# Fused cosine attention and token/channel mixer on one core: moving T4 and parts of T2 to GpSimd, another place for S1's tile, norms between exponentials, and a last product in two tiles

## The chip, the core and the metric

The kernel runs on one core of a Trainium2 chip. The core has five engines with a queue each: TensorE (PE in the profile; its weight loads are PEld), VectorE (DVE), ScalarE (ACT), GpSimd (POOL) and SyncE (SP), which issues most of the transfers. An engine takes its instructions in the order of its own queue and waits for others by semaphores. Matmul results land in PSUM, eight banks of 2 KiB per partition; everything else lives in SBUF.

The metric is the device time of one execution in microseconds (us); less is better. The time of a kernel is the median of several executions.

## The reference

Inputs in fp32: q, k, v of shape 8 x 12 x 448 x 64 (batch, heads, rows, head size), tau = 0.1 and four weight matrices.

```
q_n = q / (norm(q) + 1e-6);  k_n = k / (norm(k) + 1e-6)
attn = softmax(q_n @ k_n.T / tau)                 # 448 x 448 for each of 96 heads
x = (attn @ v), heads side by side                # 8 x 448 x 768
h = relu(x.T @ w_tok1) @ w_tok2                   # 448 -> 256 -> 448, over the rows
u = x + h.T
out = u + relu(u @ w_ch1) @ w_ch2                 # 768 -> 1536 -> 768, over the channels
```

## The kernel before

**Pairs.** Attention runs over 48 pairs of heads, six for each batch. A pair's life is spread over several turns ("slots") of one loop (line 909): its rows are loaded on SP, squared on GpSimd (`squares`), summed on VectorE (`sums`, line 266), turned into norms (`norms`: Ln and Exp on ScalarE, lines 277 and 278; a sum and a reciprocal on VectorE, lines 274 and 275), scaled to fp16 on GpSimd (`scaled`, lines 298 and 306, into a `kq` tile), transposed by a transfer on SP (`tpose_dma`, line 330, `qk<-kq`), multiplied to scores (`score`, line 345), put through exponentials on ScalarE (line 346, three of 896 columns, and line 353 for the remaining rows), and multiplied with v (`pv_rest` and `pv`, lines 367 and 384, into two `psO` banks). v is cast by GpSimd (`cast_v`, line 228). Then come the two token layers (`tok1`, line 420 with its eviction `rt` at 423; `tok2`, line 434 with its eviction `u` at 437). In slot i the scores are those of pair i and the norms and the scaling those of pair i + 2.

**Channel layers.** The two channel layers of a finished batch are cut into units (lines 467 and 483), which are put between the steps of later pairs. The loop's order is written by hand: what stands in the source is the order of each engine's queue.

**The tail.** The last two batches (B0, B1) go through the channel layers together, each layer as one 2 x 2 block product in seven block products instead of eight. For this the kernel forms sums and differences of blocks: of the first weights (`fast_weights1`: s1w, s2w, s4w, and one in place), of the second weights (`fast_weights2(n, engine)`: T1 to T4, each in three pieces of 128 x 768 fp16, each read by a later sum or a product), of u (`fast_x`: t1x to t4x) and of the hidden values (`fast_g(g, 1..4)` for each of three pairs of row tiles g; line 536 for all of them, and the tile's name tells them apart: t1g to t4g, or s1g to s4g where g is 1). The first layer's products are `p1` to `p7` (line 586), its outputs are put together by VectorE and GpSimd (`c22` on GpSimd, from two fp32 tiles) and pass a ReLU in place on ScalarE (`relu`, line 629). The second layer's products are `q1` to `q7` for each g (line 671): product 2 adds to the bank of product 1, 3 to that of 5, and 7 and 4 to that of 6, each after the bank was evicted. Last come the rows that both batches share (`shared_half`, line 735), and the stores (`store_row`, line 719).

**Order of the tail's queues before.** T1 stands on GpSimd in slot 41 (line 895). S1 stands there at the end of slot 46 (line 955), S2 on VectorE in slot 47 after the x of pair 46 (line 925), S4 on GpSimd at the end of slot 47. T2 follows t4x on GpSimd (line 991), T3 follows c22(0) (line 1001), and T4 is done by VectorE between the second layer's first and second group (line 1033).

**Memory.** The tiles of the tail are taken from a pool that opens when the pool `rest` closes in slot 45 (lines 950 to 953). `rest` held the `kq` tiles, which the transposing transfers read. In the order of allocation before, s1w lies on memory of `kq`, and so its first writer waits for the last such transfer. PSUM has two pools: `ps`, two banks (tag "b"), and `ps2`, three buffers of two banks (tag "s").

Of the kernel before, what the change touches and what calls it, by code (L numbers as in the profile page):

```python
# [22 lines left out]
def kernel(  # L23
# [511 lines left out]
    def tt(eng, out, a, b, op):  # L535
        eng.tensor_tensor(out=out, in0=a, in1=b, op=op)
# [3 lines left out]

    def tail_tiles():
        fw["t"] = {k: xtile(k, "x", [128, HD, S]) for k in (1, 2)}
        fw["s"] = [tail.tile([128, HD, C // 2], FP16, name=f"s{n}w1") for n in (1, 2, 4)]

    def xtile(k, name, shape):
        return (tail if k < 3 else tail2).tile(shape, FP16, name=f"t{k}{name}", tag=f"t{k}x", bufs=1)
# [42 lines left out]
    def etile(kind, d, bufs=1):  # L589
        e[kind, d] = (tail if kind == "e1" and d == 0 else tail2).tile([128, 2, S], FP32, name=f"{kind}_{d}", tag=kind, bufs=bufs)  # L590
        return e[kind, d][:]

    def gpart(i, b, d):
# [2 lines left out]
    def p1(d):  # L596
        bank2("X", d)
        prod1(1, d, px, True)
        nc.scalar.activation(out=etile("e1", d, 2 if d else 1), in_=px[d][:, :, 0:S], func=AF.Copy)

    def p2(d):
        prod1(2, d, px, False)
# [1 line left out]

    def p5(d):
        prod1(5, d, pz, True)
        nc.scalar.activation(out=etile("e5", d, 2), in_=pz[d][:, :, 0:S], func=AF.Copy)

    def p6(d):
        prod1(6, d, py, True)  # L610
        tt(nc.vector, etile("e16", d, 2), py[d][:, :, 0:S], e["e1", d][:], ALU.add)

    def p7(d):
        prod1(7, d, py, False)
        tt(nc.vector, etile("e167", d, 2), py[d][:, :, 0:S], e["e1", d][:], ALU.add)

    def c22(d):
        tt(nc.gpsimd, gpart(1, 1, d), e["e167", d][:], e["e5", d][:], ALU.add)
# [9 lines left out]
    def relu(i, b, d):  # L628
        nc.scalar.activation(out=gpart(i, b, d), in_=gpart(i, b, d), func=AF.Relu)

    def fast_weights2(n, eng):
        def w(i, j):
            return [wc2t[:, HC * i + 2 * m:HC * i + 2 * m + 2, DH * j:DH * (j + 1)] for m in range(3)]

        t = fw.setdefault("t2", {})
        at = [(n - 1 + m) % 2 for m in range(3)]
        t[n] = [qkv.tile([128, 2, DH], FP16, name=f"t{n}w2_{m}", tag=("qf", "kf")[z]) for m, z in enumerate(at)]
        a, b = {1: (w(0, 1), w(0, 0)), 2: (w(1, 1), t.get(1)), 3: (w(1, 1), w(0, 1)), 4: (w(1, 0), t.get(2))}[n]
        for m in range(3):
            tt(eng, t[n][m][:], a[m], b[m] if n % 2 else b[m][:], ALU.subtract)  # L640

    def fast_w2(n, j):
        if n < 4:
# [2 lines left out]
        return fw["t2"][{4: 4, 5: 1, 6: 2, 7: 3}[n]][j // 2][:, j % 2]  # L646

    TILES = ((0, 1), (2, 6), (4, 5))
    sg, xo, yo, zo, eo, orow = {}, {}, {}, {}, {}, {}

    def gtile(t, i, j0=0, j1=HC):
# [29 lines left out]
    def etile2(kind, g, bufs=2):  # L681
        eo[kind, g] = tail2.tile([128, DH], FP32, name=f"{kind}_{g}", tag=kind.replace("f", "e") if kind in ("f5", "f16", "f167") else kind, bufs=bufs)
        return eo[kind, g][:]

    def q1(g):
        xo[g] = ps.tile([128, 512], FP32, name=f"psXo_{g}", tag="b")
        prod2(1, g, xo[g], True)
        nc.scalar.activation(out=etile2("f1", g, 2), in_=xo[g][:, 0:DH], func=AF.Copy)

    def f1u(g):  # L690
        tt(nc.gpsimd, j3(etile2("f1u", g, 1)), j3(eo["f1", g][:]), urow(TILES[g][1], 0), ALU.add)
# [12 lines left out]
    def q2(g):  # L704
        orow[g] = [outp.tile([128, D], FP32, name=f"orow_{g}_{n}", tag="ost") for n in range(2)]
        prod2(2, g, xo[g], False)
        tt(nc.vector, j3(orow[g][0][:, 0:DH]), j3(xo[g][:, 0:DH]), urow(TILES[g][0], 0), ALU.add)

    def q7(g):
        prod2(7, g, yo[g], False)  # L710
# [11 lines left out]
    def q3(g):  # L722
        prod2(3, g, zo[g], False)
        tt(nc.vector, orow[g][0][:, DH:D], zo[g][:, 0:DH], eo["f16", g][:], ALU.add)
        store_row(TILES[g][0], orow[g][0])

    def q4(g, lo=0, hi=DH):
        prod2(4, g, yo[g], False, lo, hi)
        tt(nc.vector, j3(orow[g][1][:, lo:hi]), j3(yo[g][:, lo:hi]), j3(eo["f1u", g][:, lo:hi]), ALU.add)

    def shared_half(h):
        lo = DH * h
        psF = ps.tile([128, 512], FP32, name=f"psF_shared_{h}", tag="b")
        for ct in range(CT):
            nc.tensor.matmul(psF[:, 0:DH], gts[B0 // 2][:, ct, 384:512], wc2t[:, ct, lo:lo + DH],
                             start=(ct == 0), stop=(ct == CT - 1))
        o = qkv.tile([128, DH], FP32, name=f"ost_shared_{h}", tag=("qf", "kf")[h])
        (c, p0, p1_), = pieces(384, S)
        for r, b, slot in ((0, B0, 3), (64, B1, 0)):
            tt(nc.vector, j3(o[r:r + 64]), j3(psF[r:r + 64, 0:DH]), u16[b][r:r + 64, HD * h:HD * (h + 1), slot], ALU.add)  # L740
        for r, b in ((0, B0), (64, B1)):
            nc.sync.dma_start(out=out[b].rearrange("(p c) d -> c p d", c=NCH)[c, p0:p1_, lo:lo + DH], in_=o[r:r + 64])
# [21 lines left out]
    with tc.manual_schedule():  # L764
# [123 lines left out]
        def side(i):  # L888
            if i + 6 < NP_ALL and i + 2 < DMA_T0:
                load_qk(i + 6)  # L890
            cast_v(i)
            if i + 3 < NP_ALL:
                squares(i + 3)
            if i == NP_ALL - 7:
                fast_weights2(1, nc.gpsimd)
            if i in (8, 11):
                weights_ch2((i - 8) // 3)
            if i + 2 < NP_ALL:
                norms(i + 2)
                norms(i + 2, dve=True)  # L900
                scaled(i + 2)
                if i + 2 >= DMA_T0:
                    tpose_dma(i + 2)
            if i + 6 < NP_ALL and i + 2 >= DMA_T0:
                load_qk(i + 6)
            if i + 4 < NP_ALL:
                load_v(i + 4)

        for i in range(NPAIR + 1, NP_ALL):
            b, pj = i // NPAIR, i % NPAIR  # L910
            for c in range(KC):
# [12 lines left out]
            if i == NP_ALL - 1:  # L924
                fast_weights1(2, nc.vector)
            if i == NPAIR + 1:
                refill(0)
            elif pj == 2 and 1 < b < B - 1:
                refill(b - 1)
            side(i)  # L930
            if i == NP_ALL - NPAIR:
                fed[1] = (sum(t for t, _ in queue) - fed[0]) / NPAIR
            fed[0] += fed[1]
            unit(True)
            if old(i):
# [99 lines left out]
        q7(0)  # L1035
        fast_g(1, 1)
        q3(0)
        fast_g(1, 2)
        q4(0)
        store_row(TILES[0][1], orow[0][1])  # L1040
        f1u(1)
        q5(1)
        fast_g(1, 3)
        q6(1)
        fast_g(1, 4)
        q2(1)
        fast_g(2, 1)
        q7(1)
        fast_g(2, 2)
        q3(1)  # L1050
        fast_g(2, 3)
        q4(1)
        store_row(TILES[1][1], orow[1][1])
        fast_g(2, 4)
        q1(2)
        f1u(2)
        q5(2)
        q6(2)
        q2(2)
# [44 lines left out]
```

## Time and profile before

| what | us |
|---|---|
| median of 3 runs | 384.05 (383.45 to 385.09) |
| the profiled execution, device time | 384.17 |
| its span, first to last instruction | 382.4 |
| slots 44 and 45, start of scores | 301.92, 306.62 |
| slots 46 and 47, start of scores | 311.69, 318.32 |
| first layer of the tail, its first product | 322.93 |
| second layer, its first product | 350.61 |
| shared rows, first matmul | 371.98 |
| last product of the kernel (128 columns) | 377.73 |
| last store issued on SP, end | 379.58 |

The stretches of the last part, from the table of engines by window (busy us in each):

| from : to | PE | DVE | ACT | POOL | DMA GB/s |
|---|---|---|---|---|---|
| 300 : 310 | 10.00 | 7.25 | 6.42 | 7.71 | 138 |
| 310 : 320 | 9.83 | 6.05 | 4.89 | 6.28 | 128 |
| 320 : 330 | 9.40 | 8.67 | 4.56 | 6.18 | 93 |
| 330 : 340 | 10.00 | 8.15 | 4.16 | 5.17 | 0 |
| 340 : 350 | 10.00 | 7.36 | 5.48 | 9.97 | 2 |
| 350 : 360 | 8.53 | 9.74 | 5.33 | 5.82 | 1 |
| 360 : 370 | 10.00 | 8.02 | 1.47 | 6.08 | 155 |
| 370 : 383 | 7.20 | 4.61 | 0.00 | 2.74 | 95 |

A row of the order of time reads: start, length, engine, line, operation, output<-input, shape, count, and in brackets how long the engine had been idle and what ended that. Lengths of rows with a count are from the first start to the last end. The granted TensorE clock is 1.00 in every stretch up to 370 us and 0.996 over the span.

### The profile page before, as it was taken

How to read it: one execution, taken by the hardware profiler on the slowest of the kernel's cores; microseconds unless marked ns; L12 is line 12 of the kernel's file. 1: busy time of each engine (PE TensorE's matmuls, PEld its weight loads, DVE VectorE, ACT ScalarE, POOL GpSimd, SP SyncE). 2: the span in 40 equal slices, each digit the busy share in tenths (PEclk: the TensorE clock that was granted, in tenths of full speed). 3: DMA queues.
4: the chain of work that ended last, by engine and by line, in shares of the span. 5: the costliest groups of instructions: out<-in, count | busy, mean ns of one | idle time of the engine just before them, and what ended most of it. 6: DMA issues, size and time to landing. Idle time of an engine off the chain costs nothing.

```text
span 382.4 us, 10261 instructions
## 1 busy us (share of the span) xinstructions
PE 366.8 (96%) x4080; PEld 239.9 (63%) x4080; DVE 247.9 (65%) x562; ACT 234.2 (61%) x400; POOL 281.5 (74%) x411
## 2 busy tenths in 40 slices
PE   7888999989999999999999999999999999999894
PEld 6466666666667666667656666666666666655552
DVE  7789766776436574557445674556545767887973
ACT  5999887846665457845675466764676564436310
POOL 8999798978667577678567767758789867299561
PEclk9999999999999999999999999999999999999998
DMA  7999999999996898979796898967977764100234
GB/s 199 258 254 176 231 233 191 248 223 152 200 225 136 168 208 196 196 181 178 186 205 128 194 184 205 177 174 182 208 175 137 144 153 88 44 0 3 65 107 119
DMA packets 116256, 64.35 MB, mean 168 GB/s; under 512 B 72304, under 2 KB 112880, under 8 KB 116208
## 3 DMA queue, kind: packets, MB, share of 16 engines
q1 hardware_dynamic: 110224, 58.21, 72.2%
q0 software_dynamic: 5616, 5.21, 8.6%
q8 instruction: 32, 0.52, 0.6%
q10 hardware_dynamic: 368, 0.28, 0.2%
q14 instruction: 16, 0.13, 0.2%
HBM read 43.45 MB, written 11.01 MB: 142 GB/s over the span
## 4 chain that ended last, share of the span: by engine, by line
PE 78%; DVE 6%; POOL 5%; DMA 4%; ACT 3%; issue 2%; POOLq 0%; SPq 0%; DVEq 0%; ACTq 0%
PE psG L467 21%; PE psF L483 18%; PE psO L384 9%; PE psS L345 7%; PE psU L434 5%; PE psR L420 5%; PE psY L586 3%; DMA qk<-kq 2%; POOL kq L298 2%; ACT pt L346 2%; PE psYo L671 2%; PE psQ L352 2%; PE psZ L586 1%; PE psX L586 1%; DVE ssq L266 1%
## 5 line engine op out<-in xcount | busy, mean ns | idle before, releaser
L346 ACT ACTIVATE pt<-psS 128x896 f16<-128x896 f32 (+1 forms) x156 | 132.4, 917 | 53.3 <-PE psS L345 53.3
L483 PE MATMUL psF<-wc2t,gt 128*128 128x384 f16 x504 | 88.4, 326 | 0.0
L467 PE MATMUL psG<-ut,wc1t 128*128 128x448 f16 x432 | 88.1, 352 | 0.0
L298 POOL TENSOR_TENSOR kq<-kf,rn 128x384 f16<-128x384 f32 (+1 forms) x47 | 41.8, 888 | 61.5 <-DVE rn L275 59.3
L483 PEld LDWEIGHTS <-gt 128*128 128x128 f16 x504 | 47.1, 98 | 27.8
L467 PEld LDWEIGHTS <-wc1t 128*128 128x128 f16 x432 | 40.2, 98 | 32.4
L470 ACT ACTIVATE gt<-psG 128x448 f16<-128x448 f32 x72 | 38.8, 539 | 33.2 <-PE psG L467 33.2
L266 DVE TENSOR_REDUCE ssq<-sq 128x15 f32<-128x960 f32 (+2 forms) x51 | 56.2, 1102 | 3.5 <-ACT sq L248 1.9
L423 DVE TENSOR_SCALAR rt<-psR 128x256 f16<-128x256 f32 x48 | 20.1, 418 | 50.8 <-PE psR L420 50.8
L298 POOL TENSOR_TENSOR kq<-qf,rn 112x512 f16<-112x512 f32 x45 | 47.0, 1043 | 3.0
L345 PE MATMUL psS<-qk 64*128 64x448 f16 x312 | 41.7, 357 | 5.0 <-DVE qk L324 3.0
L250 POOL TENSOR_TENSOR sq<-kf 128x384 f32<-128x384 f32 (+1 forms) x46 | 40.1, 872 | 1.7 <-DMA kf<-in_k_dram 1.7
L487 DVE TENSOR_TENSOR ost<-psF,u 128x384 f32<-128x384 f32 (+1 forms) x48 | 25.6, 533 | 24.3 <-PE psF L483 21.7
L250 POOL TENSOR_TENSOR sq<-qf 112x512 f32<-112x512 f32 x39 | 40.5, 1038 | 0.0
L384 PE MATMUL psO<-vt,pt 128*128 128x65 f16 (+1 forms) x1024 | 39.2, 193 | 0.0
L388 DVE TENSOR_TENSOR x<-psO,rec 128x256 f16<-128x256 f32 x82 | 34.8, 425 | 2.8
L384 PEld LDWEIGHTS <-pt 128*128 128x128 f16 (+1 forms) x1024 | 34.2, 97 | 3.5 <-issue 0.9
L437 DVE TENSOR_TENSOR u<-psU,x 128x512 f16<-128x512 f32 x48 | 32.3, 674 | 1.9 <-PE psU L434 0.5
L434 PE MATMUL psU<-rt,w2t 128*128 128x128 f16 x384 | 29.3, 219 | 0.5 <-POOL w2t L198 0.5
L434 PEld LDWEIGHTS <-w2t 128*128 128x128 f16 x384 | 24.8, 98 | 7.9 <-issue 0.8
L420 PEld LDWEIGHTS <-w1t 128*128 128x128 f16 x384 | 24.8, 98 | 7.9 <-issue 1.8
L420 PE MATMUL psR<-x,w1t 128*128 128x128 f16 x384 | 29.3, 219 | 0.2 <-DVE u L437 0.2
(128 smaller groups left out, 477.1 us busy)
## 6 DMA issues: line engine op xcount, KB each, us to landing
qf<-in_q_dram SPq DMA_DIRECT2D x47, 224.0 KB, 4.4
kf<-in_k_dram SPq DMA_DIRECT2D x36, 192.0 KB, 3.8
vf<-in_v_dram SPq DMA_DIRECT2D x36, 192.0 KB, 3.7
vf<-in_v_dram SPq DMA_DIRECT2D x12, 224.0 KB, 8.5
kf<-in_k_dram SPq DMA_DIRECT2D x11, 224.0 KB, 8.7
wc1t<-in_moe_w_ch_dram POOLq DMA_DIRECT2D x4, 576.0 KB, 11.6
wc2t<-in_moe_w_ch_dram POOLq DMA_DIRECT2D x2, 1152.0 KB, 14.1
out_dram<-ost SPq DMA_DIRECT2D x6, 336.0 KB, 3.5
```

The lines of the kernel that those rows point to most:

```text
L250: nc.gpsimd.tensor_mul(out=dst, in0=src, in1=src)
L266: nc.vector.tensor_reduce(out=st["ssq"][0:n, sl], in_=st["sq"][0:n, sl], axis=AXX.X, op=ALU.add)
L298: eng.tensor_tensor(out=kq[0:p, a, 0:n].rearrange("p c g e -> p g c e"), in0=st["kq"[a]][:].rearrange("p (g c) e -> p g c e", g=2), in1=_b ...
L345: nc.tensor.matmul(psS[:, hh, 0:S], qk[hb, c * n:c * n + 128], qm[hb], start=True, stop=True)
L346: nc.scalar.activation(out=pts[i % 2][0:n, 2 * S * c:2 * S * (c + 1)].rearrange("p (h s) -> p h s", h=2), in_=psS[0:n, :, 0:S], func=AF.Ex ...
L384: nc.tensor.matmul(psO[:, m, 0:E + 1], pts[i % 2][0:n, at:at + 128], vt[0:n, i % HP, nch * hh + c, 0:E + 1], start=(old(i) and c == 0), st ...
L388: nc.vector.tensor_tensor(out=st["x"][:, :, hh * E:(hh + 1) * E], in0=psO[:, :, 0:E], in1=_bcast_free(rec[:], E), op=ALU.mult)
L420: nc.tensor.matmul(psR[:, tt], w1t[:, w1[m], tt * 128:(tt + 1) * 128], st["x"][:, m], start=(m == 0), stop=(m == 3))
L434: nc.tensor.matmul(psU[:, m], w2t[:, tt, lo:lo + 128], st["rt"][:, tt], start=(tt == 0), stop=(tt == TT - 1))
L467: nc.tensor.matmul(psG[:, 0:S], wc1t[:, dt, ct * 128:(ct + 1) * 128], ut[b][:, dt].rearrange("p m s -> p (m s)")[:, lo:lo + S], start=(dt ...
L470: nc.scalar.activation(out=gt[:, ct, (b % 2) * S:(b % 2 + 1) * S], in_=psG[:, 0:S], func=AF.Relu)
L483: nc.tensor.matmul(psF[:, 0:hi - lo], gt[:, ct, at:at + 128], wc2t[:, ct, lo:hi], start=(ct == 0), stop=(ct == CT - 1))
```

## The change

Five edits, all from slot 42 on:

- **T4 and T2.** `fast_weights2` loses its engine (always GpSimd) and can do single pieces. T2's first piece goes into slot 45, ahead of the scaling of pair 47; its second to the end of slot 46, ahead of S1; its third stays behind t4x. T3 follows at once, ahead of c22(0). T4 goes from VectorE to GpSimd, between c22(0) and c22(1).
- **S1's tile.** The tile e1_0 (fp32, 128 x 896) is taken from the tail's pool ahead of the S tiles, so they all move along. In the built program S1 then waits for its weights alone.
- **Norms.** In slots 42 to 45 the two ScalarE steps of the norms of pair i + 2 go from the side work after the three exponentials to a place between the second and the third. VectorE's two steps stay.
- **Order of the second layer.** Product 1 of group 1 goes ahead of product 5 of group 0. The groups become a loop: sums of the next group stand between the products of this one, and each sum goes one place ahead of the eviction that follows. The shared halves move from "b" to "s" buffers.
- **The last product.** In group 2, product 2 becomes the last of the kernel instead of product 4, and it runs in two tiles (256 and 128 columns), each with a bank of its own; product 1 of group 2, which fills these banks first, is cut likewise. Product 4 of group 2 stands between the shared halves and stores whole rows; products 3 and 7 trade places.

```diff
 def tail_tiles():
     fw["t"] = {k: xtile(k, "x", [128, HD, S]) for k in (1, 2)}
+    fw["e1"] = tail.tile([128, 2, S], FP32, name="e1_0", tag="e1")
     fw["s"] = [tail.tile([128, HD, C // 2], FP16, name=f"s{n}w1") for n in (1, 2, 4)]
...
-def fast_weights2(n, eng):
+def fast_weights2(n, parts=range(3)):
...
-    for m in range(3):
-        tt(eng, t[n][m][:], a[m], b[m] if n % 2 else b[m][:], ALU.subtract)
+    for m in parts:
+        tt(nc.gpsimd, t[n][m][:], a[m], b[m] if n % 2 else b[m][:], ALU.subtract)
...
+ENDS = ((0, 256), (256, DH))
...
-def q1(g):
-    xo[g] = ps.tile([128, 512], FP32, name=f"psXo_{g}", tag="b")
-    prod2(1, g, xo[g], True)
-    nc.scalar.activation(out=etile2("f1", g, 2), in_=xo[g][:, 0:DH], func=AF.Copy)
+def q1(g, cuts=((0, DH),)):
+    f1 = etile2("f1", g)
+    for lo, hi in cuts:
+        xo[g, lo] = ps.tile([128, 512], FP32, name=f"psXo_{g}_{lo}", tag="b")
+        prod2(1, g, xo[g, lo], True, lo, hi)
+        nc.scalar.activation(out=f1[:, lo:hi], in_=xo[g, lo][:, lo:hi], func=AF.Copy)
...
-    psF = ps.tile([128, 512], FP32, name=f"psF_shared_{h}", tag="b")
+    psF = ps2.tile([128, 512], FP32, name=f"psF_shared_{h}", tag="s")
...
         if i == NP_ALL - 7:
-            fast_weights2(1, nc.gpsimd)
+            fast_weights2(1)
+        if i == NP_ALL - 3:
+            fast_weights2(2, (0,))
...
         if i + 2 < NP_ALL:
-            norms(i + 2)
+            if i < NP_ALL - 6:
+                norms(i + 2)
             norms(i + 2, dve=True)
             scaled(i + 2)
...
         for c in range(KC):
             score(i, c)
+            if c == 1 and NP_ALL - 6 <= i < NP_ALL - 2:
+                norms(i + 2)
...
         if i == NP_ALL - 2:
+            fast_weights2(2, (1,))
             fast_weights1(1, nc.gpsimd)
...
     fast_x(3, 2, 3)
-    fast_weights2(2, nc.gpsimd)
+    fast_weights2(2, (2,))
+    fast_weights2(3)
...
     relu(1, 1, 0)
-    fast_weights2(3, nc.gpsimd)
+    fast_weights2(4)
...
     fast_g(0, 3)
+    q1(1)
+    relu(1, 1, 1)
     q5(0)
-    relu(1, 1, 1)
     relu(0, 1, 2)
     relu(1, 1, 2)
     q6(0)
     fast_g(0, 4)
-    q1(1)
-    fast_weights2(4, nc.vector)
-    q2(0)
-    q7(0)
-    fast_g(1, 1)
-    q3(0)
-    fast_g(1, 2)
-    q4(0)
...
+    for g in range(2):
+        rows(g)
+        q2(g)
+        fast_g(g + 1, 1)
+        q7(g)
+        fast_g(g + 1, 2)
+        q3(g)
+        store_row(TILES[g][0], orow[g][0])
+        fast_g(g + 1, 3)
+        q4(g)
+        fast_g(g + 1, 4)
+        if g == 0:
+            f1u(1)
+        else:
+            q1(2, ENDS)
+            f1u(2)
+        q5(g + 1)
+        q6(g + 1)
+    rows(2)
     q3(2)
+    store_row(TILES[2][0], orow[2][0], DH, D)
     q7(2)
-    store_row(TILES[2][1], orow[2][1], DH, D)
     shared_half(0)
+    q4(2)
     shared_half(1)
-    q4(2, 0, 256)
-    store_row(TILES[2][1], orow[2][1], 0, 256)
-    q4(2, 256, DH)
-    store_row(TILES[2][1], orow[2][1], 256, DH, nc.scalar)
+    for (lo, hi), eng in zip(ENDS, (nc.sync, nc.scalar)):
+        q2(2, lo, hi)
+        store_row(TILES[2][0], orow[2][0], lo, hi, eng)
```

`rows(g)` is new and only takes the two output tiles of a group; `q2` and `q4` change with it (`q2` gets the column range that `q4` had).

More of the change, by code (lines that the diff above doesn't have):

```diff
@@ L587, in prod1, with etile @@
                                  start=(start and j == 0), stop=(j == HD - 1), skip_group_check=True)
-    def etile(kind, d, bufs=1):
-        e[kind, d] = (tail if kind == "e1" and d == 0 else tail2).tile([128, 2, S], FP32, name=f"{kind}_{d}", tag=kind, bufs=bufs)
+    def etile(kind, d):
+        first = kind == "e1" and d == 0
+        e[kind, d] = fw["e1"] if first else tail2.tile([128, 2, S], FP32, name=f"{kind}_{d}", tag=kind, bufs=2)
         return e[kind, d][:]
@@ L598, in p1 @@
         prod1(1, d, px, True)
-        nc.scalar.activation(out=etile("e1", d, 2 if d else 1), in_=px[d][:, :, 0:S], func=AF.Copy)
+        nc.scalar.activation(out=etile("e1", d), in_=px[d][:, :, 0:S], func=AF.Copy)
     def p2(d):
@@ L606, in p5 @@
         prod1(5, d, pz, True)
-        nc.scalar.activation(out=etile("e5", d, 2), in_=pz[d][:, :, 0:S], func=AF.Copy)
+        nc.scalar.activation(out=etile("e5", d), in_=pz[d][:, :, 0:S], func=AF.Copy)
     def p6(d):
         prod1(6, d, py, True)
-        tt(nc.vector, etile("e16", d, 2), py[d][:, :, 0:S], e["e1", d][:], ALU.add)
+        tt(nc.vector, etile("e16", d), py[d][:, :, 0:S], e["e1", d][:], ALU.add)
     def p7(d):
         prod1(7, d, py, False)
-        tt(nc.vector, etile("e167", d, 2), py[d][:, :, 0:S], e["e1", d][:], ALU.add)
+        tt(nc.vector, etile("e167", d), py[d][:, :, 0:S], e["e1", d][:], ALU.add)
     def c22(d):
@@ L635, in fast_weights2 @@
         t = fw.setdefault("t2", {})
-        at = [(n - 1 + m) % 2 for m in range(3)]
-        t[n] = [qkv.tile([128, 2, DH], FP16, name=f"t{n}w2_{m}", tag=("qf", "kf")[z]) for m, z in enumerate(at)]
+        if n not in t:
+            at = [(n - 1 + m) % 2 for m in range(3)]
+            t[n] = [qkv.tile([128, 2, DH], FP16, name=f"t{n}w2_{m}", tag=("qf", "kf")[z]) for m, z in enumerate(at)]
         a, b = {1: (w(0, 1), w(0, 0)), 2: (w(1, 1), t.get(1)), 3: (w(1, 1), w(0, 1)), 4: (w(1, 0), t.get(2))}[n]
-        for m in range(3):
-            tt(eng, t[n][m][:], a[m], b[m] if n % 2 else b[m][:], ALU.subtract)
+        for m in parts:
+            tt(nc.gpsimd, t[n][m][:], a[m], b[m] if n % 2 else b[m][:], ALU.subtract)
     def fast_w2(n, j):
@@ L702, in q6, with rows, q2 @@
         tt(nc.gpsimd, j3(eo["f5", g][:]), j3(eo["f5", g][:]), urow(TILES[g][1], 1), ALU.add)
-    def q2(g):
+    def rows(g):
         orow[g] = [outp.tile([128, D], FP32, name=f"orow_{g}_{n}", tag="ost") for n in range(2)]
-        prod2(2, g, xo[g], False)
-        tt(nc.vector, j3(orow[g][0][:, 0:DH]), j3(xo[g][:, 0:DH]), urow(TILES[g][0], 0), ALU.add)
+    def q2(g, lo=0, hi=DH):
+        prod2(2, g, xo[g, lo], False, lo, hi)
+        tt(nc.vector, j3(orow[g][0][:, lo:hi]), j3(xo[g, lo][:, lo:hi]), urow(TILES[g][0], 0)[:, lo // 128:hi // 128], ALU.add)
     def q7(g):
@@ L724, in q3, with q4 @@
         tt(nc.vector, orow[g][0][:, DH:D], zo[g][:, 0:DH], eo["f16", g][:], ALU.add)
[L725 to L729, printed above, removed]
+    def q4(g):
+        prod2(4, g, yo[g], False)
+        tt(nc.vector, orow[g][1][:, 0:DH], yo[g][:, 0:DH], eo["f1u", g][:], ALU.add)
+        store_row(TILES[g][1], orow[g][1])
     def shared_half(h):
         lo = DH * h
-        psF = ps.tile([128, 512], FP32, name=f"psF_shared_{h}", tag="b")
+        psF = ps2.tile([128, 512], FP32, name=f"psF_shared_{h}", tag="s")
         for ct in range(CT):
@@ L1031 @@
         fast_g(0, 4)
-        q1(1)
-        fast_weights2(4, nc.vector)
-        q2(0)
-        q7(0)
-        fast_g(1, 1)
-        q3(0)
-        fast_g(1, 2)
-        q4(0)
[L1040 to L1059, printed above, removed]
+        for g in range(2):
[17 more added lines that the diff above has]
+        rows(2)
         q3(2)
+        store_row(TILES[2][0], orow[2][0], DH, D)
         q7(2)
-        store_row(TILES[2][1], orow[2][1], DH, D)
         shared_half(0)
+        q4(2)
         shared_half(1)
-        q4(2, 0, 256)
-        store_row(TILES[2][1], orow[2][1], 0, 256)
-        q4(2, 256, DH)
-        store_row(TILES[2][1], orow[2][1], 256, DH, nc.scalar)
+        for (lo, hi), eng in zip(ENDS, (nc.sync, nc.scalar)):
+            q2(2, lo, hi)
+            store_row(TILES[2][0], orow[2][0], lo, hi, eng)
 _INS = ['q', 'k', 'v', 'tau', 'moe_w_tok1', 'moe_w_tok2', 'moe_w_ch1', 'moe_w_ch2']
```

## The prediction

> **What bounds the kernel now.** I read the totals first, then TensorE's waits by window, then the order of time where the waits lie.
>
> ```profile
> span 382.4 us, 10261 instructions
> PE 366.8 (96%) x4080; PEld 239.9 (63%) x4080; DVE 247.9 (65%) x562; ACT 234.2 (61%) x400; POOL 281.5 (74%) x411
> PE psYo L671 <- DVE f L536: 1.1, 1, 1.1
> PE psYo L671 <- DVE orow L536: 1.0, 1, 1.0
> PE psO L367 <- DVE u L437: 0.5, 1, 0.5
> PE psZo L671 <- DVE t1g L536: 0.4, 1, 0.4
> PE psS L345 <- DMA qk<-kq: 0.2, 1, 0.2
> ```
>
> TensorE is busy for 96% of the span, so only its waits can be won. The five rows of waits are all that it has from 300 us on; they are single events and end 3.2 us of idle time. The end of a matmul in the trace lies some 0.16 us behind the time at which the next could start (six products of 384 columns start every 0.97 us in the chain of waits, yet the last shows as busy for 0.326), so each stall in the second layer is about 0.15 us larger than its row.
>
> ```profile
> 316.65 4.54 POOL L536 TENSOR_TENSOR s1w<-wc1t 128x2304 f16<-128x2304 f16 x1 [2.97 <-DMA qk<-kq]
> 321.14 0.50 POOL L228 CAST vt<-vf 128x384 f16<-128x384 f32 x1
> 321.22 1.63 DVE L536 TENSOR_TENSOR s2w<-s1w,wc1t 128x2304 f16<-128x2304 f16 x1 [0.31 <-POOL s1w L536]
> 324.68 0.61 PE L367 MATMUL psO<-vt,pt 64*128 64x65 f16 x8 [0.46 <-DVE u L437]
> 335.82 4.84 POOL L536 TENSOR_TENSOR t2w<-wc2t,t1w 128x768 f16<-128x768 f16 x3
> 347.54 4.13 POOL L536 TENSOR_TENSOR gt<-e,e 128x896 f16<-128x896 f32 x2
> 350.75 1.34 DVE L536 TENSOR_TENSOR t1g<-gt 128x768 f16<-128x768 f16 x1
> 352.13 0.56 DVE L536 TENSOR_TENSOR t2g<-t1g,gt 128x768 f16<-128x768 f16 x1
> 355.32 2.93 DVE L536 TENSOR_TENSOR t4w<-wc2t,t2w 128x768 f16<-128x768 f16 x3
> 359.24 1.14 PE L671 MATMUL psYo<-t4w,gt 128*128 128x384 f16 x6 [1.06 <-DVE f L536]
> 377.26 0.42 DVE L536 TENSOR_TENSOR orow<-psYo,f1u 128x256 f32<-128x256 f32 x1
> 377.73 0.49 PE L671 MATMUL psYo<-t4w,gt 128*128 128x128 f16 x6 [1.03 <-DVE orow L536]
> 377.87 1.71 SPq L719 DMA_DIRECT2D out_dram<-orow  x3
> 378.27 0.29 DVE L536 TENSOR_TENSOR orow<-psYo,f1u 128x128 f32<-128x128 f32 x1 [0.59 <-PE psYo L671]
> 378.59 0.34 ACTq L719 DMA_DIRECT2D out_dram<-orow  x1
> ```
>
> The reader is to see four places: GpSimd's 2.97 us in front of S1, VectorE's T4 (2.93 us) in front of the 1.06 us wait, the two tiles of one bank at the end, and three stores behind each other on SP.
>
> **Norms between the exponentials: 0.2 us.** In pairs 42 to 45 the Ln (0.32) and the Exp of the norm (0.22) run ahead of the third exponential, so the norms come one exponential (0.81) earlier and that exponential 0.65 later. GpSimd starts to scale pair 46 that much sooner, its transpose lands sooner, and the 0.2 us wait for `qk<-kq` goes (bounds 0 and 0.25). What hides the later exponential: in slot 43 it would end at 298.6, and TensorE takes its bank back at 299.43. The Ln would be asked for at 308.63 in slot 45, where VectorE's sum (307.22, 1.14) has ended at 308.36; margins in the other slots are 0.28 to 0.43. Behind a waiting Ln stand the third exponential and `psQ`'s. Cover gone, it costs TensorE up to the whole delay (second rival).
>
> **S1, with T2's first two pieces: 0.7 us.** One T piece is 4.84/3 = 1.61 us on GpSimd. Piece 0 now stands ahead of pair 47's scaling. Before, GpSimd idled 1.30 us there (casts end 309.28, scaling starts 310.58); with norms 0.8 sooner the casts end at 308.5, the piece at 310.1, the scaling (2.66) at 312.8 where it was 313.24. Its transpose on SP goes no later; even 1.3 us later it would be hidden, since it landed at 316.5 for scores that start at 318.32. Then the cast of v (0.46), piece 1 and S1 (4.54): S1 ends at 319.4 where it ended at 321.19. It no longer waits for the transpose, nor does anything on GpSimd behind it. S2 on VectorE stands behind the x of pair 46, which ends at 320.91; before, it had to let the cast of 321.14 pass (to 321.64) and ended at 322.85. Now it can run at 320.91 and end 0.7 us sooner. Behind it are two evictions, u (324.63) and rt (324.96), which free the two banks of `psO`. Product 1 ends at 322.93 + 6 x 0.19 = 324.07; `psO` started at 324.68 and took 0.61 against 0.30 in the slot before, so TensorE lost 0.61 + 0.31 = 0.92. With both evictions 0.7 sooner, the first bank is free in time (323.93) and the second 0.2 late: gain 0.7. Bounds: 0.3 (only VectorE's own 0.31 goes) and 0.92. e1's tile takes the memory that S1 leaves; its copy comes at 324, 7 us after the last transpose landed, and is hidden.
>
> **T4 on GpSimd, and product 1 of the second rows ahead of product 5: 1.2 us.** GpSimd runs from t4x (334.83) to the last c22 (351.67) without a gap. Two of T2's pieces leave this stretch, T4's three come in: one piece more. T2's last and T3's three now stand ahead of c22(0), so each c22 ends 1.61 later: 344.3, 351.2, and the last 353.3. Who waits: ReLUs on ScalarE and, behind them, the copies e5(1) and e5(2). They ended at 347.25 and 348.38, would end at 347.8 and 348.7, and products 3 want them at 348.34 and 349.48: hidden by 0.5 to 0.8 us; beyond that TensorE waits for every further us.
>
> Then VectorE's t1g. Its 1.34 us against 0.55 ended 0.42 after the second c22 did (351.67): two fp16 operands from SBUF stand still while GpSimd runs. T4's rows say the same: beside GpSimd's pair of additions two pieces took 1.27, the one after it 0.55. So t1g, ready at 350.75, runs when c22(1) ends, 351.2 to 351.63; c22(2) follows to 353.7, and t2g is held until then and ends at 354.1. TensorE: product 1 at 350.61, product 1 of the second rows at 351.58, product 5 at 352.56 (t1g in time, its stall of 0.57 gone), product 6 asked for at 353.53 and started at 354.15: a new stall of 0.6. Products 2, 7 and 3 follow in 0.975 each, and product 4 starts at 354.15 + 4 x 0.975 = 358.05, if the eviction of 7 is done by then; with 2.93 us of T4 gone VectorE has it at about 357.9. It was 359.24, with the same seven products before it: gain 1.2. Bounds: 1.8 if t2g slips in ahead of c22(2), 0.5 if the ReLUs of c22(2) also hold group 1's first sum, and by it the eviction of product 7, for 0.7. From product 4 to the shared rows both kernels have 17 times 0.975 us, and six more matmuls (256 + 128 columns for 384) cost nothing.
>
> The Trainium skill (SBUF — State Buffer, "Who interferes with whom") has a rule against this part: a VectorE tensor_tensor with both inputs in SBUF and a GpSimd instruction that reads SBUF exclude each other for the whole instruction. The t1g row agrees (1.34 for 0.55); if that row were only slowed by sharing, t2g would end at 353.0, no stall would come, and the sum would be 2.9 instead of 2.3.
>
> **The last product in two banks: 0.2 us.** The 1.03 us wait goes: 128 columns no longer wait for the eviction of 256. VectorE's last eviction comes right behind the one at 377.26, at 377.6 instead of 378.27. But the three stores on SP start with the 256 columns, as before at 377.87, and run 1.71 us behind each other; the last landing follows the last of these. Only ScalarE's store is 0.6 sooner for certain. Bounds 0 and 0.65; I take 0.2, nearer to SP's row. That the second rows' store of 768 columns now leaves about 1 us before the end may take that back.
>
> **Sum.** 0.2 + 0.7 + 1.2 + 0.2 = 2.3 us. The profiled execution took 384.17 us (span 382.4 and 1.77 around it), so 381.87; the median of the runs shown is 0.12 below it: 381.75. About 0.5% (1.92 us) is what a measurement of this kernel can tell from no change, so faster begins at 382.13.
>
> **Rivals.** First, the stall moves into GpSimd: every c22 is later, t2g and the ReLUs hold products 6 and 4, and the second layer gives 0.5 or nothing while the end stays bound by SP. 0.2 + 0.7 + 0 to 0.5 gives 382.7 to 383.15: no change to be told. For it: GpSimd without a gap from 334.83 and one piece more in it; against it: product 1 of the second rows covers 0.97 us. Second, slower: the Ln stands in front of the third exponential and waits for VectorE's sum. If the sum came after its full 1.14 us, the third exponential would be 0.65 + 1.14 = 1.8 late, 0.85 of it covered as in slot 43, so 0.95 in each of four slots: 3.8 lost, 1.8 won (the rest sits behind it), 386.1. It decides from a sum that ends 0.3 us or more after the second exponential and an overrun beyond 0.85; against it stand the four margins above. Third, the edits do what they say at the end as well (0.65) and t2g slips in: 0.2 + 0.9 + 1.8 + 0.65 = 3.55, 380.5.
>
> **Chances.** Forecast 0.56, first rival 0.29, third 0.07, second 0.08. Of the forecast's own range (381.0 to 382.6) about a tenth lies above 382.13. That makes faster 0.57, same 0.35, slower 0.08. The range reaches from the third rival to the first and takes the spread of the runs (383.45 to 385.09) with it: 380.3 to 383.8.
>
> **What would show it.** Right: no wait of `psS` for `qk<-kq` near 311; S1 started by a GpSimd instruction, not by a DMA, and ended before VectorE's x; `psO` after product 1 with at most 0.2 us of idle time; a t2g of about 2.5 us behind the second c22 and a wait of TensorE of half a us at product 6; at product 4 less than 0.4; three stores on SP that still start within 2 us of the last shared product. Wrong: Ln rows in pairs 42 to 45 that start late and third exponentials that TensorE waits for, or c22 rows that end after 354.5 in this clock.

## The result and the profile after

The changed kernel took 381.61 us (median of 6 runs, 380.60 to 381.96) beside 383.89 for the kernel before (6 runs, 383.45 to 385.09): ratio 0.9933, 95% interval 0.9913 to 0.9952. In a second session it was 381.91 (12 runs, 380.60 to 384.04) beside 383.17, ratio 0.9963 (0.9942 to 0.9984). Both intervals lie below 1. The medians differ by 2.3 us in the first session and by 1.3 in the second (by its interval 0.6 to 2.2), and the second session does not settle whether the gain is over half a per cent.

The totals of the changed kernel's page, and in the view of waits all of TensorE's matmuls from 300 us on (who waited for whom, us in total, times, longest):

```profile
span 378.8 us, 10270 instructions
PE 366.2 (97%) x4086; PEld 240.1 (63%) x4086; DVE 246.0 (65%) x559; ACT 234.0 (62%) x401; POOL 286.9 (76%) x414
```

```profile
PE psYo L675 <- DVE t2g L536: 0.3, 1, 0.3
```

Five rows of waits have become one. (The wait for `qk<-kq` has not gone with its row: TensorE's weight load at slot 46 still stands 0.31 us for it, 0.34 before.) The span is 3.6 us shorter, but 1.36 of that, over a third, lies ahead of slot 42, in work that the change does not touch (slot 42's first score starts at 290.47 before and at 289.11 after). So the steps are compared by the distance from slot 42's first score, in us. (Starts are read from the trace; "last shared matmul done" is its end there less the 0.16 by which such ends lie late; the columns headed "alone" are experiments told below.)

| mark | before | after | S1's tile alone | T moves alone | product 1 alone | end alone |
|---|---|---|---|---|---|---|
| slot 45 | 16.15 | 16.15 | 16.15 | 16.15 | 16.15 | 16.15 |
| slot 46 | 21.22 | 21.19 | 21.22 | 21.22 | 21.22 | 21.21 |
| first layer, second product 1 | 35.52 | 34.79 | 34.83 | 35.77 | 35.46 | 35.42 |
| second layer, first product | 60.14 | 59.43 | 59.46 | 60.39 | 60.08 | 60.04 |
| group 0's product 4 | 68.77 | 66.85 | 68.06 | 68.66 | 69.10 | 68.65 |
| last shared matmul done | 85.42 | 83.44 | 84.70 | 85.30 | 85.68 | 85.31 |
| last store starts on SP | 88.75 | 86.79 | 88.03 | 88.63 | 89.02 | 88.40 |
| end | 91.93 | 89.72 | 91.21 | 91.75 | 92.22 | 90.78 |

From slot 42 to the end the change brings 2.21: 0.03 up to slot 46, 0.70 between there and the second product 1 of the first layer, 1.21 from the second layer's first product to group 0's product 4, 0.23 behind the shared rows and 0.04 in the rest. The rows of the order of time that answer to those shown of before:

```profile
313.35 4.54 POOL L536 TENSOR_TENSOR s1w<-wc1t 128x2304 f16<-128x2304 f16 x1
...
319.43 1.35 DVE L536 TENSOR_TENSOR s2w<-s1w,wc1t 128x2304 f16<-128x2304 f16 x1
...
322.76 0.46 PE L367 MATMUL psO<-vt,pt 64*128 64x65 f16 x8
...
346.99 4.44 POOL L536 TENSOR_TENSOR gt<-e,e 128x896 f16<-128x896 f32 x2
348.68 0.82 DVE L536 TENSOR_TENSOR t1g<-gt 128x768 f16<-128x768 f16 x1
349.53 2.32 DVE L536 TENSOR_TENSOR t2g<-t1g,gt 128x768 f16<-128x768 f16 x1
...
351.91 1.15 PE L675 MATMUL psYo<-t2w,t2g 128*128 128x384 f16 x6 [0.28 <-DVE t2g L536]
...
355.96 1.14 PE L675 MATMUL psYo<-t4w,gt 128*128 128x384 f16 x6
...
373.92 0.62 DVE L536 TENSOR_TENSOR orow<-psXo,u 128x256 f32<-128x256 f32 x2
374.55 1.70 SPq L727 DMA_DIRECT2D out_dram<-orow  x3
```

S1 has no bracket any more: GpSimd comes to it straight from its other work. `psO` after product 1 shows 0.46 where it showed 0.61 behind a wait. t2g takes 2.32 where it took 0.56: VectorE stands still for it while GpSimd's second sum runs, and TensorE waits for it. At the end VectorE is done early, but three stores still take 1.70 on SP.

### The profile page after: what moved, and what is told of

It reads as the page before. It is cut to its first block, busy times and chain, and to the rows that moved or that the text cites. A ratio compares the mean times of both kernels' runs of the same rounds, so it can differ in the third digit from the quotient of the medians.

```text
span 378.8 us, 10270 instructions
## 1 busy us (share of the span) xinstructions
PE 366.2 (97%) x4086; PEld 240.1 (63%) x4086; DVE 246.0 (65%) x559; ACT 234.0 (62%) x401; POOL 286.9 (76%) x414
## 4 chain that ended last, share of the span: by engine, by line
PE 81%; DMA 7%; DVE 4%; POOL 3%; ACT 1%; issue 1%; SPq 0%; DVEq 0%; POOLq 0%
PE psG L467 21%; PE psF L483 19%; PE psO L384 9%; PE psS L345 7%; PE psU L434 5%; PE psR L420 5%; DMA qf<-in_q_dram 3%; PE psY L587 3%; PE psYo L675 2%; DMA kf<-in_k_dram 2%; PE psX L587 2%; PE psQ L352 2%; POOL kq L298 2%; PE psZ L587 2%; PE psZo L675 1%; DVE ssq L266 1%
```

## The experiments

**One part alone: S1's tile.**

```diff
+        fw["e1"] = tail.tile([128, 2, S], FP32, name="e1_0", tag="e1")
         fw["s"] = [tail.tile([128, HD, C // 2], FP16, name=f"s{n}w1") for n in (1, 2, 4)]
```

> Of the change only S1's other place in memory. My theory: S1 starts with the cast before it, about 313.7 us in the clock of before instead of 316.65, and ends near 318.2; S2 runs as soon as the x of pair 46 is done (320.9) for about 1.35 us; u and rt come 0.7 us sooner and the stop of TensorE in front of psO falls from 0.62 + 0.29 to about 0.2 us: 0.7 us gained by the second product 1 of the tail, nothing changed after it (second layer 24.6 us after that product as before). Rival: S2 itself is not what holds u; only VectorE's 0.31 us goes, and 0.3 us is gained. Time 383.2 by the theory, 383.6 by the rival.

382.85 us, ratio 0.9982 (0.9961 to 1.0003). The second product 1 comes 0.69 sooner. In the order of time of this run:

```profile
319.62 1.35 DVE L536 TENSOR_TENSOR s2w<-s1w,wc1t 128x2304 f16<-128x2304 f16 x1
...
322.95 0.45 PE L367 MATMUL psO<-vt,pt 64*128 64x65 f16 x8
```

S2 takes 1.35 for 1.63 and no longer lets a cast pass. The 0.7 stands by the marks; the time alone would not tell it from nothing.

**One part alone: the T pieces on GpSimd, product 1 of the second rows left behind product 6.**

```diff
             if i == NP_ALL - 3:
+                fast_weights2(2, (0,))
...
-        fast_weights2(4, nc.vector)
+        fast_weights2(4)
```

> Of the change only the T differences: T2's first two pieces early, T3 ahead of c22(0), T4 on GpSimd; product 1 of the second rows stays behind product 6, S1 keeps its place in memory. My theory: t2g has to wait for the second c22 and ends near 354.1 in the clock of before, while product 6 asks for it at 352.66: a new stop of about 1.5 us, which eats nearly all of the 1.8 us that T4 and t1g cost; product 4 starts 0.2 us sooner (8.4 us after the first product of the second layer instead of 8.63). T2's first piece makes the scaling of pair 47 0.3 us later, so S1 ends 0.3 later and the stop at psO grows by up to 0.3. Sum: 0 +- 0.3, time 383.9. Rival (the waits for GpSimd are a slowing, not an exclusion): t2g takes 1.3 us at most, the stop is under 0.3, product 4 starts 1.4 us sooner, time 382.6.

383.66 us, ratio 0.9990 (0.9971 to 1.0009). TensorE's wait at product 6, and the rows of the order of time behind it:

```profile
PE psYo L672 <- DVE t2g L536: 1.2, 1, 1.2
```

```profile
349.11 4.46 POOL L536 TENSOR_TENSOR gt<-e,e 128x896 f16<-128x896 f32 x2
350.81 0.83 DVE L536 TENSOR_TENSOR t1g<-gt 128x768 f16<-128x768 f16 x1
351.67 2.32 DVE L536 TENSOR_TENSOR t2g<-t1g,gt 128x768 f16<-128x768 f16 x1
```

T4 off VectorE frees product 4, but t2g behind GpSimd's second sum stops product 6 for 1.37 (with the 0.16 by which a matmul's end lies late in the trace). From the second layer's first product to product 4 it is 8.27 against 8.63: 0.36 won. Of this 0.25 is lost ahead of it: with T2's first two pieces in front of it S1 comes later, and the second product 1 of the first layer with it (35.77 against 35.52), as expected.

**One part alone: product 1 of the second rows ahead of product 5, T4 still on VectorE.**

```diff
         fast_g(0, 3)
+        q1(1)
         q5(0)
```

> Of the change only product 1 of the second rows ahead of product 5; T4 stays on VectorE. My theory: the stop of 0.57 us in front of product 5 is filled, but T4's 2.93 us on VectorE still stand in front of product 7's eviction, so the stop in front of product 4 grows by what the first one gave: product 4 starts 8.5 to 8.9 us after the first product of the second layer (8.63 before). Time 383.9. Rival (the stops add up independently): product 4 starts 0.57 us sooner, 8.06 us after, time 383.3.

384.78 us, ratio 1.0011 (0.9990 to 1.0032). The wait for t1g is gone, and the one for T4 has grown:

```profile
PE psYo L671 <- DVE f L536: 2.0, 1, 2.0
```

The stretch from the second layer's first product to product 4 takes 9.02, 0.39 more than before and a little beyond what was expected. So in this stretch one edit alone wins 0.36, the other alone loses 0.39, and both together win 1.21: product 1 covers the stop that T4's move makes, and has nothing to cover without it.

**One part alone: the end.** Products 1 and 2 of the last rows in two tiles, the shared rows from the other pool, the last stores as in the change.

```diff
-        q1(2)
+        q1(2, ENDS)
...
+        for (lo, hi), eng in zip(ENDS, (nc.sync, nc.scalar)):
+            q2(2, lo, hi)
+            store_row(TILES[2][0], orow[2][0], lo, hi, eng)
```

> Of the change only the end: product 2 of the last rows as the last product in two banks, product 4 between the shared halves, shared halves in the other PSUM pool, stores accordingly. My theory: VectorE's last eviction ends 0.6 us sooner (2.1 us after the last shared matmul instead of 2.7), but the third store on SP starts at the same distance from the last shared matmul (3.3 us), and the span ends 0 to 0.3 us sooner. Rival: the end follows VectorE's last eviction, the span ends 0.6 us sooner, time 383.3.

382.82 us, ratio 0.9973 (0.9953 to 0.9993). From the last shared matmul to the end 5.48, where before has 6.51 and the changed kernel 6.28: more than theory and rival. SP's queue in this run:

```profile
378.05 1.47 SPq L724 DMA_DIRECT2D out_dram<-orow  x3
```

The same three stores take 1.47, not 1.70, and land sooner. This set the question for the queue experiments below.

**The norms alone, and the change without them.**

```diff
-                norms(i + 2)
+                if i < NP_ALL - 6:
+                    norms(i + 2)
...
+                if c == 1 and NP_ALL - 6 <= i < NP_ALL - 2:
+                    norms(i + 2)
```

> The kernel before with the norms' move alone: in slots 42 to 45 they are sent to ScalarE after the second score instead of ahead of the scores. My step A, 0.2 us (0 to 0.25): pair 46's kq is done earlier, its DMA transpose issues 0.7 to 0.8 us earlier, the scores of slot 46 wait for it no longer, and the span is 0.2 shorter. The reading of after (only 0.04 came): the transpose is issued earlier but its issue and landing take longer (issue 2.4 to 2.5 us against 1.54), so that slot 46's scores start at most 0.05 us sooner from slot 42. Rival: what lengthened the transpose in after is other traffic or work of the change there (a piece of T2 in slot 45), and with the norms alone the issue takes 1.5 to 1.6 us and the whole 0.2 to 0.25 comes. Time 383.5 to 383.8 beside 383.8.

383.32 us, ratio 0.9972 (0.9949 to 0.9996). Slot 46 comes 0.06 sooner (21.16), as read from after, but the transpose's issue took 1.23, not 2.4: neither account holds whole. The issue's length was not what kept the gain at slot 46 small.

Behind slot 46 the norms alone do far more than either account had. The second product 1 of the first layer comes at 34.80 from slot 42, 0.72 sooner than before, and the end at 91.05, 0.88 sooner; S1's tile is where it was. The rows:

```profile
315.14 4.55 POOL L536 TENSOR_TENSOR s1w<-wc1t 128x2304 f16<-128x2304 f16 x1 [2.91 <-DMA qk<-kq]
...
323.29 0.49 PE L367 MATMUL psO<-vt,pt 64*128 64x65 f16 x8
```

S1 still waits for the last transpose, but this is issued 0.66 sooner from slot 42 (22.13 against 22.79), and S1 starts 0.72 sooner (25.46 against 26.18). It then ends ahead of the x of pair 46, S2 takes 1.38, and the wait in front of `psO` is gone. So the norms alone and S1's tile alone each bring the 0.7, and it is to be had once: both together, in the changed kernel, bring 0.73 to 0.79 up to this mark.

> The changed kernel with the norms put back ahead of the scores. If the move brings what it brought in the profile of after, the time is 0 to 0.1 above after's (381.6 to 381.7) and slot 46 starts 0.04 later from slot 42. If my step A was right after all and something else in after gave its 0.2 back, the loss is 0.2 to 0.25 (381.8 to 381.9). Rival: the move costs something that the marks do not show, since norms of a later pair now stand behind two exponentials on ScalarE, and the time without it is 0.1 to 0.3 below after's.

382.63 us, ratio 0.9964 (0.9940 to 0.9989), not in one session with after's runs, so the times are not compared. By the marks slot 46 stands at 21.23 (after: 21.19) and the end at 89.92 (89.72): no loss hidden in the move, and at most 0.2 gained by it. The second product 1 of the first layer comes at 34.84 (34.79): beside S1's tile the norms add 0.05 there.

**TensorE's code load moved: 26 more warm-up products at the start.**

```diff
-        warm(40, True)
+        warm(66, True)
```

> The changed kernel with 26 more warm-up products on TensorE at its start, which cost up to 2.8 us there (only marks from slot 42 on are read). Theory: pair 46's transpose, 0.8 us earlier since the norms moved, meets a load of TensorE's code (16384 bytes, once in 128 products, 0.9 to 1.4 us on one DMA engine from 17.9 after slot 42's start); 16 to 19 of its packets stand for 0.4 to 1.1 us until 0.8 after that load ends. 26 products more let each load come 26 products sooner, about 2 us, at 15.5 to 16.3 from slot 42. Then none of that transpose's packets takes over 0.4 us, its transfer takes 1.3 to 1.5 instead of 1.7 to 2.1, and slot 46 starts 20.98 from slot 42 (after: 21.19; the whole 0.2 of my step A). Rival: the packets stand because of the loads of inputs that the earlier transpose meets; then 16 to 19 packets still stand and the transfer takes 1.7 to 2.1 wherever the code load lies.

The DMA view of the 5 us that hold pair 46's transpose (40 slices of 0.125 us; then queues, and the transpose with its time to landing). After:

```profile
GB/s 0 0 0 0 0 0 0 131 0 0 0 10 139 205 207 207 174 72 23 8 4 12 10 10 66 285 293 283 91 0 0 295 246 295 172 221 246 246 246 295
...
q8 instruction: 1, 0.02, 1.8%
...
qk<-kq SPq DMA_TRANSPOSE x1, 3.8
```

With 26 products more:

```profile
GB/s 4 6 10 8 10 10 10 10 0 0 0 37 186 213 215 227 207 211 195 207 166 396 379 270 197 172 295 270 246 246 295 209 285 223 225 227 176 150 97 58
...
qk<-kq SPq DMA_TRANSPOSE x1, 3.1
```

After shows the transpose at 205 to 207 GB/s, then 1.0 us at 4 to 72, then the rest. The queue q8 holds one code load of 16384 bytes (by the trace's packets at 17.90 to 19.31 from slot 42; 18 packets of the transpose, begun from 18.99 on, stand until 20.12). In the other run it came at 16.18 to 17.12, no packet took over 0.14, the transpose ran through in 1.42 us, and slot 46 came at 20.98: the whole 0.2 (one run, 382.49 us, of which only marks are read). Across the other runs with the norms moved, the stop ended 0.79 to 0.90 after the code load did (loads ending at 18.88 to 19.31, slot 46 at 20.98 to 21.19). The theory holds; the rival falls, since no input is being loaded in that stretch in either run. But most of the 0.24 does not last: slot 47 comes at 27.76, 0.1 sooner than before (27.86). By the order of time the products with v now stand in slot 46 for the second bank of `psO`, which VectorE's `rt` frees at 21.66, as in the kernel before.

The same run showed something not asked for. It lost 1.5 us in the second layer, though nothing there was edited:

```profile
347.12 4.12 POOL L536 TENSOR_TENSOR gt<-e,e 128x896 f16<-128x896 f32 x2
348.80 3.73 DVE L536 TENSOR_TENSOR t1g<-gt 128x768 f16<-128x768 f16 x1
351.21 0.90 POOL L536 TENSOR_TENSOR f1u<-f,u 128x384 f32<-128x384 f32 x1
352.56 0.56 DVE L536 TENSOR_TENSOR t2g<-t1g,gt 128x768 f16<-128x768 f16 x1
```

t1g became ready at the same distance from slot 42 as in after (59.51 and 59.57) and the second sum started as there (59.89, 59.93). In after t1g slips in between GpSimd's two sums and takes 0.82; here GpSimd keeps its turn through the second sum and f1u, and t1g takes 3.73. TensorE waits 1.8 for it in product 5.

**T4's third piece back on VectorE, behind the reading of product 7's third tile.**

```diff
-        fast_weights2(4)
+        fast_weights2(4, (0, 1))
...
         p7(2)
+        fast_weights2(4, (2,), nc.vector)
```

> The changed kernel with T4's third piece taken from GpSimd and put on VectorE behind the reading of product 7's third tile; GpSimd then goes on to group 1's sums c22(1) and c22(2) some 1.6 us sooner. Theory: the wait at group 0's product 6 (0.45 us in after) is for t2g, which VectorE made in 2.32 us instead of about 0.55 because GpSimd's two sums c22 held the other end of their reads; with those done sooner t2g takes 0.5 to 0.9 us, the wait at product 6 is under 0.1, and the time is 0.35 to 0.5 below after's (381.1 to 381.25). Rival: the wait only moves, because the third piece on VectorE is itself slowed and pushes VectorE's next readings back, and the time is within 0.15 of after's.

381.30 us (6 runs, 380.74 to 381.73), ratio 0.9927 (0.9899 to 0.9954).

```profile
346.60 4.12 POOL L536 TENSOR_TENSOR gt<-e,e 128x896 f16<-128x896 f32 x2 [0.34 <-ACT e L609]
349.49 1.64 DVE L536 TENSOR_TENSOR t1g<-gt 128x768 f16<-128x768 f16 x1
351.09 0.91 POOL L536 TENSOR_TENSOR f1u<-f,u 128x384 f32<-128x384 f32 x1 [0.37 <-ACT f L694]
351.17 1.25 DVE L536 TENSOR_TENSOR t2g<-t1g,gt 128x768 f16<-128x768 f16 x1
```

Half right. The first of the two sums is done when t1g wants to run and the second is running, so t1g waits for that one alone and takes 1.64, but t2g now meets f1u and takes 1.25 instead of the 0.5 to 0.9 expected. The wait at product 6 falls from 0.45 to 0.2 and product 4 comes 0.25 sooner (7.18 against 7.43 from the second layer's first product).

**The last 16-row piece on ScalarE.**

```diff
-            store_row(TILES[2][0], orow[2][0], lo, hi, eng)
+            store_row(TILES[2][0], orow[2][0], lo, hi, eng, rest)
```

(`rest` is ScalarE for the 256-column store; `store_row` sends every piece but the first there.)

> The changed kernel with the 16-row second piece of the last 256-column store sent by ScalarE instead of SyncE, so that SyncE sends two and ScalarE two of the last four stores. Step D of the prediction: SyncE's three stores in a row bind the end, so the last store starts 0.4 to 0.7 us sooner from the last shared product and the time falls by as much (380.9 to 381.2). Rival: the end is bound by the landing on the DMA engine that also loads 8192 bytes of code about 3.6 us after the last shared product (0.6 to 0.7 us of that engine); the last store starts sooner, but the end of the span from the last shared product stays within 0.2 of after's 6.28 unless that load moves too.

381.78 us, ratio 0.9940 (0.9914 to 0.9966). The last store on SP starts 3.00 after the last shared matmul (after: 3.35) and the end is at 5.97 (6.28). That lies between the two accounts: SP's queue gives 0.3, not 0.4 to 0.7.

**SP's queue six instructions longer.**

```diff
+        if hi - lo == D and t in HALVED:
+            cut = [(c, q, q + (p1_ - p0) // 2) for c, p0, p1_ in cut for q in (p0, p0 + (p1_ - p0) // 2)]
```

> The changed kernel with six of the stores of groups 0 and 1 cut in two, so that SyncE's queue is six instructions longer ahead of the last stores; nothing else moves. Theory: SyncE stops for 0.37 to 0.39 us ahead of its 463rd instruction, and a code load of 8192 bytes follows as it passes the 466th; in the changed kernel these lie between its last three stores and within their landing. Six instructions more put them at 0.1 to 1.4 us after the last shared product, where SyncE waits for the eviction anyway, as they lay in the run of the end alone. Then SyncE's last store starts 2.95 to 3.15 us after the last shared product (3.35 in after), the span ends 5.4 to 5.7 after it (6.28), and the time falls by 0.5 to 0.8 (380.8 to 381.1). Rival: the end of the end-alone kernel came from its other order of work and not from the place of the code load: then the last store starts at 3.3 to 3.4, the span ends 6.2 to 6.3 after the last shared product, and the time is within 0.2 of after's.

381.53 us, ratio 0.9958 (0.9928 to 0.9987). SP's last stores in this run, and the queue of code loads in the DMA view from 0.7 to 2.8 us after the last shared matmul:

```profile
375.71 1.47 SPq L731 DMA_DIRECT2D out_dram<-orow  x3
```

```profile
q14 instruction: 1, 0.01, 0.9%
```

In after that load lies at 3.68; here it comes at 1.39, and takes 0.31 us instead of 0.58. The last store starts at 3.10, as expected, and the rival falls. The end is at 5.84, 0.4 sooner than after but 0.14 later than expected: of SP's nine closing waits, which take about 0.06 each, the second held here until 4.42 with seven behind it, where the end alone had passed six by 3.97.

**The last three edits together, and the change again on the same chip.**

> The changed kernel with three edits at once: T4's third piece on VectorE, the 16-row piece of the last 256-column store on ScalarE, and the six stores cut in two. If the three add up: no wait at product 6, the last shared product 0.3 sooner, the span's end 5.0 to 5.4 us after it instead of 6.28, and a time 1.1 to 1.5 below after's (380.1 to 380.5). Rival: the landing of the shared output's stores binds the end once SyncE no longer does, the span ends 5.6 or more after the last shared product, and the time is at most 0.9 below after's (380.7 or more).

381.04 us (7 runs, 380.63 to 381.81), ratio 0.9943 (0.9922 to 0.9963). The last store starts 2.62 after the last shared matmul, but the end is at 5.79: the rival's figures for the end and the time, though not by its cause. The shared output's stores had landed by 3.80; SP's closing waits pass at 4.18 and 4.53, when stores of the last rows landed (4.17 and 4.51). The wait at product 6 is 0.2 and not gone. From slot 42 to the end 88.94, 0.78 less than in after.

> The changed kernel as it is, beside the three above on the same chip. Expected 381.3 to 381.9, ratio 0.993 to 0.995; its profile with the norms' gain between 0.03 and 0.25 at slot 46 by the length of the code load there, the wait at product 6 at 0.4 to 0.5, and the end 6.2 to 6.4 us after the last shared product. Rival, that its gain beyond 0.5% was chance: ratio 0.996 or more.

381.91 us, ratio 0.9963 (0.9942 to 0.9984), on the rival's side of 0.996, with an interval that covers both theory and rival. In its profile slot 46 came at 20.98, the wait at product 6 was 0.46 and the end 6.32 behind the shared rows. The three edits together lie below both kernels by the medians; from the kernel before they are told apart, from the changed one not yet, since the intervals overlap.

## Why the prediction came out as it did

381.75 was forecast and 381.61 measured. The sum of 2.3 stands against 2.21 by the marks of the profile. That they agree so closely is in part luck: the terms of the norms and of S1 overlap, and that of the end varies from one execution to the next.

- **Norms, 0.2: the first step is right, the price is not.** The 0.8 us by which pair 46's transpose goes out sooner are there, and no exponential was late (slots 43 to 45 agree within 0.01, so the second rival fell). But "its transpose lands sooner" held for 0.04 us of the 0.8 in the profile of after: moved forward, it ran into a load of TensorE's code, which I had not looked for among the transfers. At slot 46 the gain is 0.03 to 0.24, by the time at which that load ends (its length does not decide: 0.88 us with a gain of 0.06 in one run, 1.18 with 0.24 in another); at slot 47 0.04 to 0.10 of it are left. The sum priced the move by slot 46's wait alone. What it does to the next transpose, and so to S1, was not in it: alone it brings 0.72 there.
- **S1, 0.7: right in size and in its path, but not the tile's alone.** 0.70 in after and 0.69 alone; S1 ends ahead of VectorE's x as foretold. The norms' move reaches the same 0.7 without the tile. The two terms were added as if they were independent; beside the tile the norms add 0.1 at most. What the tile adds beside the norms and the T2 pieces was not run.
- **T4 with product 1, 1.2: right, with its parts.** 1.21; product 4 came 7.42 behind the second layer's first product where 7.44 had been worked out, t2g's 2.32 and the stop of 0.45 stand for the "about 2.5" and 0.6. That one edit needs the other is shown by the two alone. What I took as settled is not: that t1g runs between GpSimd's sums. It did so in five of the six profiles of this order, and in the sixth it cost 1.5. The first rival (0 to 0.5 from the second layer) fell, and t2g slipped in nowhere, so the third did too.
- **The end, 0.2: right by its reason, its size one execution's.** VectorE's last eviction ends 0.67 sooner behind the shared rows, the last store on SP does not (3.33 and 3.35); 0.23 comes from the landing. That varies: in the five profiles with the old end (before and four parts) the span ends 6.37 to 6.54 after the last shared matmul, in the five with the new end and SP's queue as in after 6.28 to 6.55, on average 0.1 less. What holds SP there is more than three issues in a row: a stop of 0.37 between its last stores and the code load belong to it.

The rule of the Trainium skill (SBUF — State Buffer, "Who interferes with whom") that spoke against the third step is borne out: t2g took 2.32 instead of 0.56 and t1g once 3.73, waits of whole GpSimd instructions and no slowing in proportion.

Open: the changed kernel's later runs reach 384.04, and of its 18 runs and the 28 of three variants with the same order of T4 16 lie above 382.5, while the 13 runs of the two kernels with T4's third piece on VectorE reach 381.81 at most. A lost turn of t1g would account for 1.5 us of that; it was seen in one profile only, and one long run (385.37) was late ahead of slot 42 instead. But the kernel before, in which no other GpSimd instruction is ready behind the sum that t1g waits for, spreads as far in the same two sessions (382.69 to 386.00 and 382.27 to 385.08). So this is possible and not shown.

## What to carry to other kernels

A stop removed from one engine is worth what the next one to arrive leaves of it: try the parts of a change singly and in pairs. A cover such as product 1 here can cost 0.4 us alone and add 0.85 in company, and two edits such as the norms and S1's tile can each be worth 0.7 us alone and hardly more together. Follow an instruction that moves to everything that waits for its results, and not only to the wait that it was moved for. Where VectorE and GpSimd both work on operands in SBUF, lay out their order so that no instruction on the path has to win a turn between two of the other's. Compare profiles from a mark ahead of the change, not by their spans: here a third of the difference was not the change's.

## What was not expected of the hardware

- **Code loads share the DMA engines with the kernel's transfers.** TensorE's are 16384 bytes each, 32 in 4086 products, so one in 128; 0.9 to 1.4 us in the stretch looked at here. The Trainium skill (Advanced Engine Details and Errata, "ISA Cache") gives a line of 16 KB as 256 instructions, and 128 products with their weight loads are that. SP's loads are 8192 bytes, half of it.
- **A transpose stops almost as a whole behind one.** 17 to 19 of its 1024 packets stood for up to 1.1 us, until 0.79 to 0.90 us after the code load ended.
- **SP stops for 0.37 to 0.39 us at a fixed place of its program**, behind 463 recorded instructions in all fourteen profiles, and a load of code follows 0.6 to 1.15 us after its end. Six instructions more moved both by 2.3 to 2.5 us, away from the last stores.
- **Turns between VectorE and GpSimd are not decided by who is ready first.** With the same starts to within 0.06 us, t1g took 0.82 once and 3.73 another time.
